# Tokens and weights of both feed-forward layers' first multiplication as pairs of fp16 tiles, with scales found on the chip

## The chip, the cores and the metric

The program runs on one core of a Trainium2 chip. The metric is the device time of the launch in microseconds (us). The core has five engines: TensorE (PE in the profile, its weight loads are PEld), VectorE (DVE), ScalarE (ACT), GpSimd (POOL) and SyncE (SP, which here only issues DMAs). Each works through its own queue in order.

## The reference

Attention with mixing of heads ahead of and behind the softmax, then two feed-forward layers, all in float32. After attention there are 4 x 448 = 1792 tokens of 768 numbers.

```
scores = q @ k^T / 8;  scores = mix_pre(scores);  attn = softmax(scores)
x = mix_post(attn) @ v                       # 1792 x 768
h = x @ w_in;  x = (h * cos(h)) @ w_out      # layer 0: 768 -> 2048 -> 768
g = x @ w_gate;  v = x @ w_val
out = (silu(g) * v) @ w_out2                 # layer 1: 768 -> 1536 -> 768
```

## The kernel before

**Precision.** A float32 product is made from three matmuls of a high and a low part: each operand `a` is split into `hi`, `a` rounded to a type that TensorE takes, and `lo = a - hi`, and `wh*xh + wh*xl + wl*xh` goes into one PSUM tile. In the feed-forward layers both parts are fp32r, a 4-byte type. The softmax and `post` part of attention already uses fp16 parts.

**Attention** runs from 0 to about 515 us as one list of steps for 180 blocks, whose order on every engine is written out by hand (`order`, L360, under `tc.manual_schedule`). In the last chunk of blocks the start of layer 0 is woven in by `early_plan` (L629).

**Feed-forward layers** (`run`, L652). The hidden dimension is cut into groups of 256 columns (8 groups in layer 0, 6 in layer 1), the tokens into 4 tiles `t` of 448. A unit is one group and one token tile: `l1` (L593) makes 2 x 128 hidden columns (`e` = 0, 1), with 18 matmuls of 448 columns each (6 blocks of 128 rows, three products; L567 to L569), in layer 1 twice that, for gate and value (`col`). `hidden` (L571) makes the nonlinearity and splits the result into `gh` and `gl`. `l2` (L600) multiplies it with 2 x 128 rows of the second weight matrix: 6 output tiles `m`, 6 matmuls each (L613 to L615), and each PSUM tile `py` (pool `ps_y`, four buffers) is added into `acc` in SBUF (L619 on VectorE, for the first group a copy on ScalarE, L617). `l2` of a unit stands one unit behind its `l1`. In the last group of layer 0 each finished `acc` tile is split at once into the next layer's tokens (L622, L623).

**Weights** arrive as 64-bit words, the bits of float64 numbers. `w_dma` (L463) loads half a slab, 3 blocks of 128 x 128, into `raw` (three buffers). `w_shift` (L473, ScalarE) scales the upper words, `w_bits` (L482, three VectorE instructions) puts the float32 number together from both words, and `w_split` (L494) makes `hi` (L506, ScalarE) and `lo` (L507, GpSimd). A slab of the first multiplication has key `(layer, "i", col, fi)`, one of the second `(layer, "o", fi)`. The half-built number `f` has two buffers. `load_in` (L514) is written ahead of the unit or units that need it: in layer 0 in the first unit of a group, for the next group; in layer 1 behind the `l2` that follows the last `l1` of a group, right ahead of the next group's first `l1`.

**Order.** Outside the block written by hand, the framework orders each engine's queue while the kernel is built. The place in the program is the priority; an instruction whose inputs are expected later lets later ones pass. What came of it for this kernel is seen in the trace.

**Scale of v.** `scale_v` (L147) finds a power of two for the values `v`, by a maximum, a matmul with `ones` (tile psp, L76), and arithmetic on exponents. `pv_out` (L290) takes it out again (`und`) when attention's result leaves PSUM.

## Time and profile before

| | |
|---|---|
| median of 3 runs | 1530.59 us (1526.16 to 1532.99) |
| the profiled execution | 1526.95 us, span 1525.2 us |
| mean granted clock of TensorE | 0.994 of full speed |
| busy | PE 1452.0, PEld 1199.3, DVE 971.4, ACT 652.4, POOL 632.0 us |
| stages | attention to about 515 us, layer 0 to about 975, layer 1 to the end |

The span goes from the first to the last instruction of the program; the profiled execution took 1.75 us more than that. Times in the rows are counted from the start of the span. The end of a matmul is modelled and neighbours overlap, so the distance from one start to the next, not the duration, says how fast TensorE goes. Releasers, what ended an engine's idle time, are inferred from semaphores.

### The profile page before, as it was taken

To read this page: it belongs to the slowest core of one execution; us is meant where nothing else is said; L and a number is where in the kernel's file an instruction comes from. 1 tells how busy PE (TensorE), PEld (TensorE's weight loads), DVE (VectorE), ACT (ScalarE), POOL (GpSimd) and SP (SyncE) were. 2 spreads that over 40 slices of the span, in tenths; PEclk is the share of its full clock that TensorE was granted. 3 is DMA by queue.
4 is the path that set the end of the run, shared out by engine and by line. 5 is a ranking of instruction groups with operands and counts; after the bars stand their busy time and mean duration, and the time that the engine had idled before them with its cause. 6 is when DMAs were issued, how large, how long until landed. Compare 5 with 4: busy or idle time off the path is not lost.

```text
span 1525.2 us, 26832 instructions
## 1 busy us (share of the span) xinstructions
PE 1452.0 (95%) x10306; PEld 1199.3 (79%) x10306; DVE 971.4 (64%) x1982; ACT 652.4 (43%) x1398; POOL 632.0 (41%) x531
## 2 busy tenths in 40 slices
PE   4799899999998799999999999999999999999999
PEld 2465566565566699999999998998998989899898
DVE  3888788889889684866766767834236263543613
ACT  3677777777776562322322323534313131221310
POOL 1777677777768542432322422313223131321310
PEclk9999999999999999999999999999999999999999
DMA  5445445455445530211202211202102030120202
GB/s 169 132 135 161 141 138 164 142 150 156 137 120 148 149 118 21 84 42 42 83 21 63 65 39 42 82 23 67 58 20 85 21 104 22 55 70 0 73 37 109
DMA packets 93567, 133.04 MB, mean 87 GB/s; under 512 B 18848, under 2 KB 80768, under 8 KB 93440
## 3 DMA queue, kind: packets, MB, share of 16 engines
q1 hardware_dynamic: 93440, 131.34, 29.0%
q8 instruction: 81, 1.33, 0.4%
q14 instruction: 46, 0.38, 0.1%
HBM read 81.59 MB, written 11.01 MB: 61 GB/s over the span
## 4 chain that ended last, share of the span: by engine, by line
PE 57%; DVE 4%; POOL 2%; ACT 1%; issue 1%; ACTq 0%; POOLq 0%
PE ph L568 11%; PE ph L567 11%; PE ph L569 11%; PE py L613 8%; PE py L614 8%; PE py L615 8%; POOL l_i L507 1%; DVE f_i L490 1%; DVE f_i L487 1%; DVE f_i L486 1%; ACT f_i L479 1%; ACT h_i L506 0%; POOL l_o L507 0%; DVE f_o L486 0%; DVE r L589 0%
## 5 line engine op out<-in xcount | busy, mean ns | idle before, releaser
L567 PE MATMUL ph<-x,h_i 128*128 128x448 f32 x960 | 352.5, 367 | 0.0
L569 PE MATMUL ph<-x,l_i 128*128 128x448 f32 x960 | 350.7, 365 | 0.9 <-POOL l_i L507 0.9
L568 PE MATMUL ph<-x,h_i 128*128 128x448 f32 x960 | 350.6, 365 | 0.7 <-POOL x L547 0.7
L591 POOL TENSOR_TENSOR gl<-r,gh 128x448 fp32r<-128x448 f32 x112 | 134.0, 1196 | 498.1 <-ACT gh L590 468.0
L231 POOL TENSOR_SCALAR eh<-e,sm 120x448 f16<-120x448 f32 x180 | 246.7, 1371 | 129.3 <-DVE sm L226 91.0
L613 PE MATMUL py<-gh,h_o 128*128 128x448 f32 x672 | 249.9, 372 | 13.0 <-DVE acc L619 7.9
L615 PE MATMUL py<-gh,l_o 128*128 128x448 f32 x672 | 247.8, 369 | 3.0 <-POOL l_o L507 3.0
L614 PE MATMUL py<-gl,h_o 128*128 128x448 f32 x672 | 247.5, 368 | 0.0
L619 DVE TENSOR_TENSOR acc<-py,acc 128x448 f32<-128x448 f32 x288 | 175.8, 619 | 88.2 <-PE py L615 87.9
L202 PE MATMUL psm<-x,wpre_sb 120*120 120x448 f32 x360 | 179.5, 581 | 15.1 <-ACT e L215 14.9
L568 PEld LDWEIGHTS ph<-x,h_i 128*128 128x128 f32 x960 | 180.3, 188 | 16.2 <-POOL x L547 1.1
L569 PEld LDWEIGHTS ph<-x,l_i 128*128 128x128 f32 x960 | 180.2, 188 | 16.2 <-POOL l_i L507 1.6
L567 PEld LDWEIGHTS ph<-x,h_i 128*128 128x128 f32 x960 | 180.3, 188 | 15.6 <-issue 0.6
L589 DVE TENSOR_TENSOR r<-ph,r 128x448 f32<-128x448 f32 x48 | 29.9, 623 | 198.9 <-PE ph L569 198.7
L613 PEld LDWEIGHTS py<-gh,h_o 128*128 128x128 f32 x672 | 126.5, 188 | 32.0 <-DVE acc L619 13.1
L507 POOL TENSOR_TENSOR l_i<-f_i,h_i 128x384 fp32r<-128x384 f32 x80 | 86.8, 1092 | 139.0 <-ACT h_i L506 139.0
L251 PE MATMUL psa<-wpost,eh 120*112 120x120 f16 x720 | 131.6, 226 | 13.0 <-DVE at L272 10.3
L615 PEld LDWEIGHTS py<-gh,l_o 128*128 128x128 f32 x672 | 126.6, 188 | 15.9 <-POOL l_o L507 4.1
L590 ACT CAST gh<-r 128x448 fp32r<-128x448 f32 x112 | 63.4, 566 | 173.2 <-DVE r L589 135.0
L215 ACT ACTIVATE e<-psm,sm 120x448 f32<-120x448 f32 x180 | 115.2, 640 | 50.5 <-DVE sm L226 48.9
L614 PEld LDWEIGHTS py<-gl,h_o 128*128 128x128 f32 x672 | 126.6, 188 | 11.4
L238 DVE SCALAR_TENSOR_TENSOR el<-e,sm,eh 120x448 f16<-120x448 f32 x180 | 133.4, 741 | 1.4 <-POOL eh L231 1.4
(83 smaller groups left out, 2320.5 us busy)
## 6 DMA issues: line engine op xcount, KB each, us to landing
r_o<-in_w_out SPq DMA_DIRECT2D x56, 384.0 KB
x<-s SPq DMA_DIRECT2D x96, 210.0 KB
r_i<-in_w_in SPq DMA_DIRECT2D x32, 384.0 KB
x<-s SPq DMA_DIRECT2D x48, 192.5 KB
r_i<-in_w_gate SPq DMA_DIRECT2D x24, 384.0 KB
r_i<-in_w_val SPq DMA_DIRECT2D x24, 384.0 KB
x<-s SPq DMA_DIRECT2D x48, 175.0 KB
qr<-in_qT SPq DMA_DIRECT2D x15, 360.0 KB
```

What stands on the lines that cost most here:

```text
L202: nc.tensor.matmul(ps[:120, :S], wpre_sb, X[b, c][:120, k], start=True, stop=True)
L231: nc.gpsimd.tensor_scalar(eh, E[b, c, k], sm[:, 3:4], 1.0, op0=ALU.mult, op1=ALU.mult)
L238: nc.vector.scalar_tensor_tensor(el, E.pop((b, c, k)), sm[:, 3:4], eh, op0=ALU.mult, op1=ALU.subtract)
L251: nc.tensor.matmul(o, eh[:, j], wpost_sb[0], start=True, stop=False)
L567: nc.tensor.matmul(ps, wh, xh, start=(kk == 0), stop=False)
L568: nc.tensor.matmul(ps, wh, xl, start=False, stop=False)
L569: nc.tensor.matmul(ps, wl, xh, start=False, stop=(kk == 5))
L591: nc.gpsimd.tensor_tensor(gl, r, f(gh), op=ALU.subtract)
L613: nc.tensor.matmul(ps, wh, gh[:, e], start=(e == 0), stop=False)
L614: nc.tensor.matmul(ps, wh, gl[:, e], start=False, stop=False)
L615: nc.tensor.matmul(ps, wl, gh[:, e], start=False, stop=(e == 1))
L619: nc.vector.tensor_tensor(acc[:, m], ps, acc[:, m], op=ALU.add)
```

## The change

The tokens X of both layers and the weight slabs of the first multiplication (`"i"`) are now pairs of fp16 tiles. So that the parts keep enough bits, each weight slab and each token tile is brought to a suitable size by a power of two, found on the chip:

- `w_max` takes the largest magnitude of each partition from the upper words of a raw half slab (VectorE). `w_sum` reduces the two halves' maxima to a power of two on each partition and adds these up over the partitions with a matmul of `ones` by one column; `w_unit` cuts the sum to a power of two and makes its inverse, which `w_shift` then uses as scale. So nothing of a slab is built before both its halves have landed and the matmul is through.
- For the tokens of layer 0 the scale is that of v, which `pv_out` now leaves in. For layer 1, `l2` of the last group takes the maximum of each `acc` tile, and `next_x` makes the scale in the same way, behind all six tiles, and then splits them.
- `hidden` takes the scales out again, by a scalar for each partition (`w_by`), in instructions that were there, of which one changes its form.
- One of the four `py` buffers in PSUM becomes the place of the sums (`ps_u`). `raw` (and the other default tiles of its pool) gets five buffers instead of three.
- In `early_plan` the loads and steps of the first two slabs move.

```diff
+    ff.ones = ones
+    ff.ps_sum = lambda name: ps_v.tile([128, 512], F32, tag="pv", name=name)
...
             p = pow2_c(scales[b], 112, f"v{b}")
-            und = const.tile([128, 1], F32, tag="und", bufs=2, name=f"und_{b}")
-            nc.vector.tensor_scalar(und, p[:, 0:1], pw[:, 0:1], 2.0 ** -14, op0=ALU.mult, op1=ALU.mult)
-            vscale[b] = p, und
+            nc.vector.tensor_scalar(
+                ff.unit[0][:, b:b + 1], p[:, 0:1], pw[:, 0:1], 2.0 ** -9, op0=ALU.mult, op1=ALU.mult
+            )
+            vscale[b] = p
...
-        nc.scalar.activation(x, PV.pop((b, c, g3))[:, :3, :n], AF.Copy, scale=vscale[b][1])
+        nc.scalar.activation(x, PV.pop((b, c, g3))[:, :3, :n], AF.Copy, scale=2.0 ** -5)
...
-        self.p_wr = self.pool("m_wr", 3, side="right")
+        self.p_wr = self.pool("m_wr", 5, side="right")
...
-        self.ps_y = self.pool("ps_y", 4, PSUM)
+        self.ps_y = self.pool("ps_y", 3, PSUM)
+        ps_u = self.pool("ps_u", 1, PSUM)
+        self.ps_sum = lambda name: ps_u.tile([128, 512], F32, tag="u", name=name)
...
+    def w_max(self, key, z):
+        if z == 0:
+            self.scale[key] = self.p_unit.tile([128, 6], F32, tag="u", name="u_" + self.nm(key, z))
+        top = self.raw[key, z].bitcast(F32).rearrange("p m (n w) -> p (m n) w", w=2)[:, :, 1]
+        self.tc.nc.vector.tensor_reduce(
+            out=self.scale[key][:, z:z + 1], in_=top, axis=AX.X, op=ALU.max, apply_absolute_value=True
+        )
+    def w_sum(self, key):
+        nc = self.tc.nc
+        u = self.scale[key]
+        m = u[:, 2:3]
+        nc.vector.tensor_scalar(m, u[:, 0:1], u[:, 1:2], 2.0 ** -112, op0=ALU.max, op1=ALU.mult)
+        nc.vector.tensor_scalar(
+            m.bitcast(I32), m.bitcast(I32), 3, 0x7C000000, op0=ALU.logical_shift_left, op1=ALU.bitwise_and
+        )
+        ps = self.ps_sum("su_" + self.nm(key, 0))
+        nc.tensor.matmul(ps[:, 0:1], self.ones, m, start=True, stop=True)
+        self.part["sum", key] = ps
+    def w_unit(self, key):
+        nc = self.tc.nc
+        u = self.scale[key].bitcast(I32)
+        ps = self.part.pop(("sum", key))[:, 0:1].bitcast(I32)
+        nc.vector.tensor_scalar(u[:, 3:4], ps, 0x7C000000, None, op0=ALU.bitwise_and)
+        nc.vector.tensor_scalar(
+            u[:, 4:5], u[:, 3:4], 3, 31 << 23, op0=ALU.logical_shift_right, op1=ALU.bitwise_xor
+        )
...
         t = self.p_wr.tile([128, 3, 128], F32, tag="f", bufs=2, name="f_" + self.nm(key, z))
-        nc.scalar.activation(t, top, AF.Copy, scale=2.0 ** -112)
+        by = self.scale[key][:, 4:5] if key[1] == "i" else 2.0 ** -112
+        nc.scalar.activation(t, top, AF.Copy, scale=by)
         self.part[key, z] = t
...
+            kind = F16 if key[1] == "i" else F32R
             self.W[key] = tuple(
-                pool.tile([128, 6, 128], F32R, tag=tag + p, name=p + "_" + self.nm(key, z)) for p in "hl"
+                pool.tile([128, 6, 128], kind, tag=tag + p, name=p + "_" + self.nm(key, z)) for p in "hl"
             )
+            if key[1] == "i" and (key[0] == 0 or key[3] > 1):
+                self.w_by(key)
         hi, lo = (w[:, 3 * z:3 * z + 3] for w in self.W[key])
         t = self.part.pop((key, z))
         nc.scalar.copy(hi, t)
-        nc.gpsimd.tensor_tensor(lo, t, f(hi), op=ALU.subtract)
+        nc.gpsimd.tensor_tensor(lo, t, hi if key[1] == "i" else f(hi), op=ALU.subtract)
+    def w_by(self, key, t=None):
+        nc = self.tc.nc
+        layer = key[0]
+        if t in (None, 0):
+            self.by[key] = self.p_unit.tile([128, 2, 4], F32, tag="by", bufs=6, name="by_" + self.nm(key, 0))
+        ts = slice(0, 4) if t is None else slice(t, t + 1)
+        for i, c in enumerate((0.5, 0.5 * INV2PI) if layer == 0 else (0.5,)):
+            nc.vector.tensor_scalar(
+                self.by[key][:, i, ts], self.unit[layer][:, ts], self.scale[key][:, 3:4], c,
+                op0=ALU.mult, op1=ALU.mult,
+            )
...
     def load_w(self, key):
+        if key[1] == "i":
+            for step in (self.w_dma, self.w_max):
+                for z in range(2):
+                    step(key, z)
+            self.w_sum(key)
+            self.w_unit(key)
         for z in range(2):
-            for step in (self.w_dma, self.w_shift, self.w_bits, self.w_split):
+            if key[1] == "o":
+                self.w_dma(key, z)
+            for step in (self.w_shift, self.w_bits, self.w_split):
                 step(key, z)
...
-            x = self.p_x.tile([128, 12, S], F32R, tag="x", name=f"x{layer}_{t}")
+            x = self.p_x.tile([128, 12, S], F16, tag="x", name=f"x{layer}_{t}", padded_shape=[128, 24, S])
...
-            self.p_hl[t].tile([128, 6, S], F32R, tag=f"hl{z}", name=f"x{layer}{z}_{t}") for z in range(2)
...
-        eng.tensor_tensor(lo, self.raw.pop(("x", t, m)), f(hi), op=ALU.subtract)
...
+            by, turn = (self.by[0, "i", 0, 2 * g + e][:, i, t:t + 1] for i in range(2))
...
-            nc.vector.tensor_scalar(k, ps, INV2PI, 0.25, op0=ALU.mult, op1=ALU.add)
-            nc.vector.scalar_tensor_tensor(r, ps, INV2PI, k, op0=ALU.mult, op1=ALU.subtract)
+            nc.vector.tensor_scalar(k, ps, turn, 0.25, op0=ALU.mult, op1=ALU.add)
+            nc.vector.scalar_tensor_tensor(r, ps, turn, k, op0=ALU.mult, op1=ALU.subtract)
...
-            nc.vector.tensor_tensor(r, ps, r, op=ALU.mult)
+            nc.vector.scalar_tensor_tensor(r, ps, by, r, op0=ALU.mult, op1=ALU.mult)
         else:
-            nc.scalar.activation(r, self.PH[e, 0], AF.Silu)
-            nc.vector.tensor_tensor(r, self.PH[e, 1], r, op=ALU.mult)
+            if g == 0:
+                for col in range(2):
+                    self.w_by((1, "i", col, e), t)
+            by = [self.by[1, "i", col, 2 * g + e][:, 0, t:t + 1] for col in range(2)]
+            nc.scalar.activation(r, self.PH[e, 0], AF.Silu, scale=by[0])
+            nc.vector.scalar_tensor_tensor(r, self.PH[e, 1], by[1], r, op0=ALU.mult, op1=ALU.mult)
...
-            self.x_new(1, t)
+            mx = self.p_unit.tile([128, 8], F32, tag="mx", bufs=2, name=f"mx_{t}")
...
             if last and layer == 0:
-                hi, lo = (x[:, m] for x in self.X[1, t])
-                nc.scalar.copy(hi, acc[:, m])
-                nc.vector.tensor_tensor(lo, acc[:, m], f(hi), op=ALU.subtract)
+                nc.vector.tensor_reduce(
+                    out=mx[:, m:m + 1], in_=acc[:, m], axis=AX.X, op=ALU.max, apply_absolute_value=True
+                )
             elif last:
...
+        if last and layer == 0:
+            self.next_x(t, acc, mx)
+    def next_x(self, t, acc, mx):
+        nc = self.tc.nc
+        self.x_new(1, t)
+        u, by = mx[:, 6:7], mx[:, 7:8]
+        nc.vector.tensor_reduce(out=u, in_=mx[:, :6], axis=AX.X, op=ALU.max)
+        ps = self.ps_sum(f"sx_{t}")
+        nc.tensor.matmul(ps[:, 0:1], self.ones, u, start=True, stop=True)
+        nc.vector.tensor_scalar(u, ps[:, 0:1], 2.0 ** -100, 2.0 ** 100, op0=ALU.max, op1=ALU.min)
+        nc.vector.tensor_scalar(u.bitcast(I32), u.bitcast(I32), 0x7F800000, None, op0=ALU.bitwise_and)
+        nc.vector.tensor_scalar(self.unit[1][:, t:t + 1], u, 2.0 ** -14, None, op0=ALU.mult)
+        nc.vector.reciprocal(by, self.unit[1][:, t:t + 1])
+        for m in range(6):
+            hi, lo = (x[:, m] for x in self.X[1, t])
+            nc.scalar.activation(hi, acc[:, m], AF.Copy, scale=by)
+            nc.vector.scalar_tensor_tensor(lo, acc[:, m], by, hi, op0=ALU.mult, op1=ALU.subtract)
...
-        wi = (0, 0, 0, 0), (1, 3, 6, 8)
+        wi = (0, 0, 1, 2), (3, 4, 6, 8)
...
             plan.append((s + wi[0][k], self.w_dma, key, z))
+            plan.append((s + wi[0][k] + 1, self.w_max, key, z))
+            if z:
+                plan.append((s + wi[0][k] + 2, self.w_sum, key))
+                plan.append((s + wi[0][k] + 3, self.w_unit, key))
```

## Rows read from the trace of the kernel before

**Rows 1.** The page, busy time and share of each engine.

```profile
PE 1452.0 (95%) x10306; PEld 1199.3 (79%) x10306; DVE 971.4 (64%) x1982; ACT 652.4 (43%) x1398; POOL 632.0 (41%) x531
```

**Rows 2.** Windows: stretch, its length; busy us (instructions) per engine, clock, DMA share, GB/s.

```profile
455.00:505.00 50.00, 43.56 (x549) 32.14 (x548) 46.06 (x101) 32.93 (x75) 38.30 (x29) 0.97 0.50 149
555.00:870.00 315.00, 315.00 (x1536) 286.96 (x1534) 213.19 (x379) 100.77 (x186) 99.72 (x87) 1.00 0.19 58
945.00:1005.00 60.00, 60.00 (x295) 54.95 (x294) 49.43 (x90) 29.55 (x55) 17.46 (x15) 1.00 0.20 61
1005.00:1045.00 40.00, 40.00 (x198) 36.84 (x197) 2.50 (x4) 10.19 (x19) 4.63 (x4) 1.00 0.03 10
```

**Rows 3.** Waits of PE over the run: us in total, times, longest.

```profile
PE py L613 <- DVE acc L619: 7.9, 10, 1.0
```

**Rows 4.** The page, groups: count | busy us, mean ns | idle before, releaser.

```profile
L567 PE MATMUL ph<-x,h_i 128*128 128x448 f32 x960 | 352.5, 367 | 0.0
```

**Rows 5.** Timeline of PE in layer 1, then layer 0: start us, us.

```profile
1089.81 0.36 PE L568 MATMUL ph<-x,h_i 128*128 128x448 f32 x1
...
1090.21 0.36 PE L567 MATMUL ph<-x,h_i 128*128 128x448 f32 x1
...
623.68 0.37 PE L569 MATMUL ph<-x,l_i 128*128 128x448 f32 x1
...
624.72 0.37 PE L568 MATMUL ph<-x,h_i 128*128 128x448 f32 x1
```

**Rows 6.** Timeline of PE, `post` of one block: first and last of twelve.

```profile
41.46 0.22 PE L251 MATMUL psa<-wpost,eh 120*112 120x120 f16 x1
...
42.04 0.22 PE L253 MATMUL psa<-wpost,el 120*112 120x120 f16 x1
```

**Rows 7.** Timeline of PE around the sum for v's scale.

```profile
43.95 0.37 PE L76 MATMUL psp_v<-diag_v,ones 112*128 112x112 f32 x2
44.25 0.68 PE L186 MATMUL pss<-k,q 64*120 64x448 f32 x4
```

**Rows 8.** Groups of DVE instructions by form.

```profile
L140 DVE TENSOR_REDUCE vmx<-vm 112x1 f32<-112x768 f32 x16 | 15.1, 943 | 0.5 <-DMA vm<-in_vN 0.5
...
L584 DVE SCALAR_TENSOR_TENSOR r<-ph,k 128x448 f32<-128x448 f32 x64 | 39.7, 620 | 1.5
...
L222 DVE TENSOR_SCALAR sm<-sm 120x1 f32<-120x1 f32 x180 | 26.4, 147 | 56.9 <-ACT e L215 56.7
```

**Rows 9.** Timeline of DVE and PE in two bursts of layer 0.

```profile
616.34 1.14 DVE L619 TENSOR_TENSOR acc<-py,acc 128x448 f32<-128x448 f32 x2
...
616.49 0.37 PE L613 MATMUL py<-gh,h_o 128*128 128x448 f32 x1
...
631.78 0.61 DVE L619 TENSOR_TENSOR acc<-py,acc 128x448 f32<-128x448 f32 x1
...
631.30 0.37 PE L613 MATMUL py<-gh,h_o 128*128 128x448 f32 x1
```

**Rows 10.** Timeline at a change of group in layer 1, and DVE later.

```profile
1046.28 1.99 POOL L507 TENSOR_TENSOR l_i<-f_i,h_i 128x384 fp32r<-128x384 f32 x2 [8.85 <-ACT h_i L506]
...
1047.33 0.55 ACT L479 ACTIVATE f_i<-r_i 128x384 f32<-128x384 f32 x1 [0.28 <-POOL l_i L507]
...
1050.49 1.02 POOL L507 TENSOR_TENSOR l_i<-f_i,h_i 128x384 fp32r<-128x384 f32 x1 [2.23 <-ACT h_i L506]
...
1063.88 1.33 POOL L507 TENSOR_TENSOR l_i<-f_i,h_i 128x384 fp32r<-128x384 f32 x1
...
1065.53 0.36 PE L615 MATMUL py<-gh,l_o 128*128 128x448 f32 x1
1065.73 0.36 PE L567 MATMUL ph<-x,h_i 128*128 128x448 f32 x1
...
1089.43 0.58 DVE L486 TENSOR_SCALAR f_i<-f_i 128x384 int32<-128x384 int32 x1 [8.12 <-ACT f_i L479]
```

**Rows 11.** The chain that ended last: start us, us, what.

```profile
1135.78 1.02 POOL l_i L507
```

More of the change, by code (lines that the diff above doesn't have):

```diff
@@ L61, in attention @@
     ps_m = pool("ps_m", 2, PSUM, mixed)
-    ones = const.tile([128, 128], F32, name="ones")
+    ones = ff.p_const.tile([128, 128], F32, name="ones")
     nc.vector.memset(ones, 1.0)
@@ L164, in split_v @@
         rv = r.rearrange("p (m e d) -> p m e d", e=2, d=D)
-        by = vscale[b][0][:112, 1:2]
+        by = vscale[b][:112, 1:2]
         if part == 0:
@@ L358, in attention @@
         at(i, fn, *a)
-    order = ("at_hi","l1_part","post","spread","dma_v","w_bits","hidden","den","rowmax","rec","norm_hi","dma_k","x_dma","w_dma","pv_out","at_lo","norm_lo","lo_k","dma_q","max_v","w_shift","lo_q","split_v","x_lo","premix","scale_v","w_split","expo","x_hi","qk","hi_k","hi_q","pv")
+    order = ("at_hi","l1_part","post","spread","dma_v","w_sum","w_unit","w_bits","hidden","den","rowmax","rec","norm_hi","dma_k","x_dma","w_dma","pv_out","at_lo","norm_lo","lo_k","dma_q","max_v","w_max","w_shift","lo_q","split_v","x_lo","premix","scale_v","w_split","expo","x_hi","qk","hi_k","hi_q","pv")
     with tc.manual_schedule():
@@ L422, in __init__ @@
         self.p_x = self.pool("m_x", 2)
+        self.p_const = self.pool("m_const", 1)
+        self.p_unit = self.pool("m_unit", 4)
+        self.unit = [self.p_const.tile([128, 4], F32, name=f"unit{layer}") for layer in range(2)]
+        self.scale, self.by = {}, {}
         cols = [w.rearrange("(k p) n -> p k n", p=128) for w in (w_in, w_gate, w_val)]
@@ L530, in x_new @@
         self.X[layer, t] = tuple(
-            self.p_hl[t].tile([128, 6, S], F32R, tag=f"hl{z}", name=f"x{layer}{z}_{t}") for z in range(2)
+            self.p_hl[t].tile([128, 6, S], F16, tag=f"hl{z}", name=f"x{layer}{z}_{t}") for z in range(2)
         )
@@ L546, in x_lo @@
         eng = self.tc.nc.vector if t and m % 2 else self.tc.nc.gpsimd
-        eng.tensor_tensor(lo, self.raw.pop(("x", t, m)), f(hi), op=ALU.subtract)
+        eng.tensor_tensor(lo, self.raw.pop(("x", t, m)), hi, op=ALU.subtract)
     def load_x(self, t):
```

## Prediction, made before the changed kernel was run

> **What bounds the kernel now.** I read the page first: its busy line and its clock line say whether one engine fills the span. TensorE (PE) is busy for 1452.0 of 1525.2 us, nobody else for more than two thirds [rows 1]. Busy time flatters PE, because the records of pipelined matmuls overlap, so next I read busy time by stretch [rows 2]. From 555 to 870 us PE has no gap at all, at the full granted clock, and runs 1536 matmuls in 315 us, 205 ns each. The attention tail (455 to 505) is another stage: there PE has gaps and VectorE (DVE) is busy for 46.06 of 50 us. Third, the waits of PE: over the whole run the largest total in the feed-forward layers is 7.9 us, behind the additions into `acc` [rows 3]. So in the feed-forward layers, about two thirds of the run, the spacing of the matmuls sets the time. What matters is the step from one start to the next, not the recorded duration (367 ns).
>
> **The matmuls that change.** The first multiplication has 3 x 960 = 2880 matmuls of 448 columns (three lines, L567 to L569, of which one row is shown) [rows 4]. Their starts lie 200 ns apart in a quiet stretch of layer 1 (two steps from 1089.81 to 1090.21) and 208 ns apart in a busy one of layer 0 (623.68 to 624.72: five steps in 1.04 us) [rows 5]. I take 203.5, near the middle. The trace has no fp16 matmul of this width, but `post` has fp16 ones of 120 columns, each with a weight load of its own: 11 steps in 0.58 us (41.46 to 42.04), 52.7 ns each [rows 6]. 120 columns at the granted 2.4 GHz are 50 ns, so an fp16 matmul with its load costs 2.7 ns beside its columns, where a 4-byte one costs 13 to 21 ns beside 186.7. An fp16 matmul of 448 columns should come to 52.7 + 328 / 2.4 = 189.4 ns. Bounds: 186.7 (columns alone), and 200 to 208 (no change). Gain: 2880 x (203.5 - 189.4) = 40.6 us; from 0 to 49.
>
> One rule speaks against that. The `post` rows show 52.7 ns with a new weight tile each time. The Trainium skill ("TensorE: Matmul & The Clock Gate", section "Weight-path perf modes — Fast Weight Load (FWL) and DoubleRow") says that the array takes one element per cell and cycle whatever its width, and that the weight load goes by columns and not bytes; the same section says that a faster weight load is on for 128 weights of a type that isn't FP32. By the first sentence alone nothing is gained; by the second the load shrinks. The measured 4-byte step of 200 to 208 is longer than its columns, and the `post` step isn't, so the trace sides with the second.
>
> **What PE gets in addition.** One sum over partitions for each of 40 weight slabs (16 in layer 0, 24 in layer 1) and for each of 4 token tiles: `ones` (128x128, f32) against one column. The nearest rows are the two psp records: the first starts at 43.95, the next other matmul at 44.25, 0.30 us [rows 7]. They move 112 columns twice (2 x 47 ns); without these some 0.2 us stay. 44 x 0.2 = 8.8 us; bounds 2 x 53 ns (two smallest steps with a load each, 4.7 us in all) and 0.30 us (13.2).
>
> **What DVE gets.** Each half slab a maximum over 384 elements. A reduction of 768 takes 943 ns and an instruction on one element 147 [rows 8]; that is 1.04 ns an element, so 147 + 384 x 1.04 = 0.55 us, x 80 = 44 us. The token maxima (448) are 24 x 0.61 = 15 us. Small instructions: 4 for each slab (160), 68 for `w_by`, 20 in `next_x`, at 0.15 us [rows 8], 38 us. Together 97 us on 971 [rows 1]. The operations of `hidden` and `next_x` that change form keep their price: with one operand from PSUM, the fused form (L584) takes 620 ns and the plain addition (L619) 0.61 us [rows 8, 9]. ScalarE and GpSimd get the same counts with 2-byte outputs: nothing, and ScalarE's idle time would cover some. Where is DVE's cover? From 555 to 870 it is idle for 102 of 315 us [rows 2], and the new work there (some 4 us for each of 5 to 6 pairs of slabs) fits. Two places lack cover:
> - Attention tail: 4 halves and 2 slabs fall in it, 2.2 + 12 x 0.15 = 4 us, against 3.9 us of idle DVE [rows 2]. I take 3 us (0 to 4); the new maxima also wait for DMAs that only ScalarE waited for, with rowmax behind them on DVE.
> - Between the layers: `next_x` and the token maxima bring 15 + 3 us, while DVE is idle for 10.6 of 60 us from 945 to 1005, and for 37.5 of 40 behind that [rows 2]. 7 us have no cover at once, the rest can slide. I take 5 us (0 to 8).
>
> **Three PSUM buffers for py instead of four.** With three, the fourth tile of `l2` waits for the first tile's addition. In two bursts of one group I can read that off: the fourth tile's first matmul starts at 616.49, the first tile's addition at 616.34 (two end at 617.48, so the first near 616.9), 0.4 us late; in the second burst they are at 631.30 and 631.78 (to 632.39), 1.1 us late [rows 9]. For 7 groups of layer 0 that is 7 x 1.5 = 10.5 us, 12 with some room. I take 6: a PE that has waited once lets DVE catch up, and five raw buffers instead of three let the work on the slabs spread. In layer 1 the present waits behind `acc` grow by at most one tile (1.23 us) at each of 5 changes of group; I take 4 us (0 to 6).
>
> **The longer chain to a weight slab.** Maximum, sum, unit, then as before. In layer 1 a slab set's splitting begins at 1046.28 (GpSimd's first l_i) and ends with the one at 1063.88 (1.33 long); the matmuls that use it begin at 1065.73 [rows 10]. The last slab is needed only after three quarters of 14 us more. The chain grows by about 2 us a slab (two maxima, four small instructions, a turn on PE), 8 us for four, and the slack of over 10 us hides it, if its sums run as early as the trace shows other steps to run: the bit work at 1089.43 belongs to a group whose splitting the chain of waits shows at 1135.78 [rows 10, 11]. I take 2 us (0 to 4). SP's queue has the same DMAs, no more; the maxima now hold up only what comes later on DVE.
>
> **Sum.** -40.6 + 8.8 + 3 + 5 + 6 + 4 + 2 = -11.8 us, on the profiled execution's 1526.95 us (1.75 beside its span): 1515.2. The three timed runs have a median of 1530.59, 3.6 above it, and that difference is no property of the change; I give 1517, in between and nearer to the sum.
>
> **Rivals.**
> - *The sum waits for its place on PE (slower).* Everywhere in layer 1, PE goes in program order: the second multiplication ends with its matmul at 1065.53, the next unit's first starts at 1065.73 [rows 10]. `load_in` for the next group of layer 1 stands right ahead of the unit that needs it. If PE never runs dry earlier, the sums run only there, and splitting starts there and not 18 us earlier. From then: 0.7 us (sum, unit) + 4.1 (ScalarE shift, three DVE steps, cast, GpSimd: 1047.33 to 1051.51) + 17.9 (1047.33 to 1065.21, six halves more [rows 10]) = 22.7 us to the last half. PE has 7.4 us of `l2` and about 12 us of `l1` ahead of that, so it waits 3 us, and the three further sums wait for DVE in its busiest stretch, another 2. Six changes of group: 30 us, less the 2 above: 1545. It decides from a start later than 19 us ahead of the last need. For it: PE's gapless order. Against: DVE's and ScalarE's queues do run ahead.
> - *DVE gives everything back (no change).* The buffer and boundary terms at their upper bounds (12 + 6 + 8 + 4) and the sums at 13.2: -40.6 + 13.2 + 30 + 2 = +4.6, 1532. For it: DVE's back-to-back rows in bursts [rows 9].
> - *Half the gain.* The 4-byte step of a quiet stretch is 200, and what disturbs the busy one stays: 2880 x 10.6 = 30.5 us instead of 40.6: 1527.
> - *The type doesn't matter.* The change then doesn't bring what it could: 1517 + 40 = 1557. Against it: the `post` step [rows 6]. The skill's sentence on element width is this rival.
> - *All covers hold*: -40.6 + 4.7 + 3 = -33, 1494 to 1498.
>
> **From these to the numbers.** Chances: forecast 0.40, sum at its place 0.24, DVE gives all back 0.13, half the gain 0.12, type 0.05, covers 0.06. The forecast itself spans 1508 to 1526; the range, with the first rival inside and the last two mostly outside, is 1499 to 1548. A measurement tells about 0.5% (7.6 us) from no change. Faster: 0.35 of the forecast, 0.06, 0.04 of the half gain, 0.02: 0.47. Slower: 0.21 of the first rival, 0.05 of the type, 0.06 of DVE: 0.32. Same: 0.21.
>
> **What would show it.** In the profile after, starts of the first multiplication's matmuls about 189 ns apart (over 198: the type rival). Two sum records and about 0.2 us beside the stream. Waits of PE on `acc` of 15 to 20 us in all (more: DVE). Waits of the sum matmul or of ph on l_i: a few us; at about 5 us each at 1/6 of layer 1, the first rival. DVE near 1070 us busy. The prediction is wrong if PE's waits in layer 1 exceed 15 us, or if the step isn't below 195 ns.

## The result: slower, 1.0132 times the time before, and the profile after

The changed kernel takes 1549.01 us (median of 4, 1547.83 to 1551.89) against 1528.8 us of the kernel before, run beside it: ratio 1.0132, 95% interval 1.0103 to 1.0162. The forecast was 1517 with a range up to 1548. Its profiled execution took 1547.83 us, with a span of 1545.7.

I read the views in the order of the prediction. The busy line of the page, answering to [rows 1]:

```profile
PE 1436.3 (93%) x10394; PEld 943.8 (61%) x10394; DVE 1048.3 (68%) x2334; ACT 663.8 (43%) x1398; POOL 622.0 (40%) x531
```

PE is less busy than before in a longer span, weight loads have shrunk by 255 us, and DVE has 77 us more, where the prediction said 97. Busy time by stretch, the same stretches and columns as [rows 2], changed kernel:

```profile
555.00:870.00 315.00, 297.02 (x1482) 207.32 (x1480) 223.90 (x433) 98.01 (x174) 87.33 (x81) 0.98 0.17 51
945.00:1005.00 60.00, 58.30 (x295) 43.68 (x294) 50.69 (x106) 19.80 (x35) 11.11 (x10) 1.00 0.00 1
1005.00:1045.00 40.00, 34.41 (x165) 17.66 (x166) 36.81 (x92) 21.01 (x38) 16.52 (x15) 0.91 0.41 118
```

In the stretch of layer 0 where PE had no gap, it now has 18 us of them and starts 54 matmuls fewer. The clock has a part in the fewer starts: behind 520 us the trace has TensorE at 1.2 GHz for 20.5 us, before for 3.4. The longest such stretch, 10.2 us from 590 us on, lies behind waits for an out slab. Two windows of it (columns as above; 0.50 of the clock is 1.2 GHz):

```profile
585.00:590.00 5.00, 2.85 (x14) 1.59 (x13) 4.52 (x8) 2.08 (x5) 2.28 (x2) 1.00 0.52 158
595.00:600.00 5.00, 3.98 (x11) 2.63 (x11) 3.89 (x7) 1.74 (x3) 3.24 (x3) 0.50 0.41 122
```

So look at what PE waits for. Waits of PE in the changed kernel from 520 us on (total us, times, longest):

```profile
PE ph L638 <- POOL l_i L555: 13.8, 32, 0.8
PE py L687 <- ACT h_o L554: 11.2, 13, 2.5
PE py L689 <- POOL l_o L555: 7.4, 13, 1.9
PE py L687 <- DVE acc L693: 6.9, 8, 1.3
PE ph L636 <- ACT h_i L554: 4.3, 2, 4.1
```

Before, the largest was `acc` with 7.9 [rows 3], and these two, 6.7 us in all, were the waits on weight slabs:

```profile
PE py L613 <- ACT h_o L506: 3.7, 1, 3.7
PE py L615 <- POOL l_o L507: 3.0, 3, 2.1
```

`acc` hasn't grown. The waits on weight slabs have, to 36.7 us. Those in layer 0 (18.6 us) are all on out slabs (`h_o`, `l_o`), those in layer 1 (18.1) all on in slabs (`h_i`, `l_i`), the ones that now need a sum. The matmuls themselves do what was forecast. PE's timeline in layer 0, changed kernel, first and last of fourteen:

```profile
757.72 0.35 PE L637 MATMUL ph<-x,h_i 128*128 128x448 f16 x1
...
760.18 0.35 PE L638 MATMUL ph<-x,l_i 128*128 128x448 f16 x1
```

13 steps in 2.46 us are 189.2 ns each; before it was 200 to 208 [rows 5]. Over the run, the mean step between starts (disturbed ones of 215 ns and more left out) is 189.7 ns in layer 0 and 189.5 in layer 1, against 203.2 and 202.6.

Why the slabs are late is seen where the sums lie. Timeline of the changed kernel in layer 0, DVE, PE and ACT, for the two in slabs of one group:

```profile
716.10 0.54 DVE L488 TENSOR_REDUCE u_i<-r_i 128x1 f32<-128x384 f32 x1
...
728.57 0.54 DVE L488 TENSOR_REDUCE u_i<-r_i 128x1 f32<-128x384 f32 x1
...
760.37 0.28 PE L503 MATMUL su_i<-u_i,ones 128*128 128x1 f32 x2
...
761.24 0.15 DVE L512 TENSOR_SCALAR u_i<-su_i 128x1 int32<-128x1 int32 x1
...
761.61 0.28 PE L503 MATMUL su_i<-u_i,ones 128*128 128x1 f32 x2
...
762.72 0.63 ACT L524 ACTIVATE f_i<-r_i,u_i 128x384 f32<-128x384 f32 x1
```

All maxima are there at 729, and the small steps behind them at 731. The sums run at 760.37 and 761.61, behind the first `l1` of the group, which is the place of `load_in` in the program. For over 30 us nothing of the slabs can be built; then eight halves, the out slabs' among them, go through ACT, DVE and POOL at once, and PE waits for the out slabs, which it needs first. In layer 1 the sums lie behind an `l2` (1180.87 and 1182.11, then 1191.99 and 1195.81), and the `l1` that uses the slabs runs beside their building. PE's and POOL's timeline there:

```profile
1180.87 0.28 PE L503 MATMUL su_i<-u_i,ones 128*128 128x1 f32 x2
...
1190.93 0.36 PE L638 MATMUL ph<-x,l_i 128*128 128x448 f16 x1 [0.39 <-POOL l_i L555]
...
1202.93 0.36 PE L638 MATMUL ph<-x,l_i 128*128 128x448 f16 x1 [0.61 <-POOL l_i L555]
...
1203.94 1.28 POOL L555 TENSOR_TENSOR l_i<-f_i,h_i 128x384 f16<-128x384 f32 x1 [1.06 <-ACT h_i L554]
1205.27 0.36 PE L638 MATMUL ph<-x,l_i 128*128 128x448 f16 x1 [0.47 <-POOL l_i L555]
```

The splitting of the set ends at 1205, 24 us behind the first sum. Before, it began 19 us ahead of the first use [rows 10]. This is what the first rival described for layer 1. Its 1545 comes nearest of all, but by luck, as the account of the steps below shows; and the late sum isn't the whole cause, as the experiments show.

### The profile page after: what moved, and what is told of

The parts are those of the page before. It is cut to its first block, busy times and chain, and to the rows that moved or that the text cites. A ratio compares the mean times of both kernels' runs of the same rounds, so it can differ in the third digit from the quotient of the medians.

```text
span 1545.7 us, 27273 instructions
## 1 busy us (share of the span) xinstructions
PE 1436.3 (93%) x10394; PEld 943.8 (61%) x10394; DVE 1048.3 (68%) x2334; ACT 663.8 (43%) x1398; POOL 622.0 (40%) x531
## 4 chain that ended last, share of the span: by engine, by line
PE 44%; DVE 7%; POOL 5%; ACT 3%; issue 2%; DMA 0%; POOLq 0%; DVEq 0%; ACTq 0%; SPq 0%
PE ph L638 9%; PE ph L636 8%; PE ph L637 8%; PE py L689 6%; PE py L687 6%; PE py L688 6%; POOL l_i L555 3%; DVE f_i L532 2%; ACT f_i L524 1%; ACT h_i L554 1%; DVE f_i L531 1%; DVE f_i L535 1%; POOL l_o L555 1%; DVE f_o L532 1%; POOL gl L665 1%
## 5 line engine op out<-in xcount | busy, mean ns | idle before, releaser
L638 PE MATMUL ph<-x,l_i 128*128 128x448 f16 x960 | 340.4, 355 | 18.3 <-POOL l_i L555 18.2
L636 PE MATMUL ph<-x,h_i 128*128 128x448 f16 x960 | 341.9, 356 | 7.2 <-ACT h_i L554 4.3
L665 POOL TENSOR_TENSOR gl<-r,gh 128x448 fp32r<-128x448 f32 x112 | 134.2, 1198 | 526.0 <-ACT gh L664 522.9
L637 PE MATMUL ph<-x,h_i 128*128 128x448 f16 x960 | 340.5, 355 | 0.7 <-DVE x L616 0.7
L687 PE MATMUL py<-gh,h_o 128*128 128x448 f32 x672 | 256.6, 382 | 20.2 <-ACT h_o L554 11.2
L638 PEld LDWEIGHTS <-l_i 128*128 128x128 f16 x960 | 94.4, 98 | 120.7 <-POOL l_i L555 34.7
L636 PEld LDWEIGHTS <-h_i 128*128 128x128 f16 x960 | 95.1, 99 | 98.1 <-issue 14.2
L663 DVE SCALAR_TENSOR_TENSOR r<-ph,by_i,r 128x448 f32<-128x448 f32 x48 | 32.7, 680 | 177.5 <-PE ph L638 177.5
L637 PEld LDWEIGHTS <-h_i 128*128 128x128 f16 x960 | 94.4, 98 | 84.2 <-issue 6.2
L555 POOL TENSOR_TENSOR l_i<-f_i,h_i 128x384 f16<-128x384 f32 x80 | 77.5, 977 | 149.9 <-ACT h_i L554 145.8
L200 ACT COPY s<-pss 120x448 f32<-120x448 f32 (+2 forms) x192 | 96.8, 536 | 83.2 <-DMA x<-s 34.0
```

The source lines that it names most:

```text
L555: nc.gpsimd.tensor_tensor(lo, t, hi if key[1] == "i" else f(hi), op=ALU.subtract)
L636: nc.tensor.matmul(ps, wh, xh, start=(kk == 0), stop=False)
L637: nc.tensor.matmul(ps, wh, xl, start=False, stop=False)
L638: nc.tensor.matmul(ps, wl, xh, start=False, stop=(kk == 5))
L665: nc.gpsimd.tensor_tensor(gl, r, f(gh), op=ALU.subtract)
L687: nc.tensor.matmul(ps, wh, gh[:, e], start=(e == 0), stop=False)
```

## The experiments

Several runs change one thing and see the loss move elsewhere, so the explanations came one behind another. The expectations name them by letters. A: the sums' place alone. B: VectorE's added work itself. C: three `py` buffers. D: a burst of slab work is paid once, in slabs when they are late or in `acc` when they are early. E and H: in that burst the two `f` buffers chain the engines. F: the loss sits in PE's own pace. The others are explained where they stand. "Before" in each comparison was run beside the experiment. The framework orders all queues anew for each kernel, so a small edit also moves other instructions, and a difference of a few us between two kernels has that in it. Of the code only the lines that matter are shown; `...` stands for others.

**e1, no sums for the slabs.** The changed kernel with the fixed scale of the kernel before for slabs; their maxima, sums and scales are left out. The tokens' stay.

```diff
-        by = self.scale[key][:, 4:5] if key[1] == "i" else 2.0 ** -112
+        by = 2.0 ** -112
...
```

> The changed kernel with a fixed scale for the weight slabs (2^-112, as the second multiplication has it) in place of the one found on the chip: maxima, sums and units of the 40 slabs are left out, the tokens' scales stay. Theory A (the sums sit at their place in the program on PE, the weight slabs start late, PE waits for them): the waits on l_i, h_o, l_o and h_i (18.2 + 11.2 + 7.4 + 4.3 = 41 us) fall to about 8 as before, the 40 sums go too (6 us): 1549 - 33 - 6 = about 1510. Rival B (VectorE's added work holds up everything): most of the 97 us of VectorE work goes, so about 1510 as well; e2_unused tells A and B apart. Rival C (three py buffers): they stay, so not under 1535.

Measured: 1544.0 us, 1.0101 [1.006, 1.0141]. Only 5 us came back. PE's waits in e1, from 520 us on:

```profile
PE py L683 <- DVE acc L689: 37.7, 20, 4.9
PE py L683 <- ACT acc L687: 7.0, 4, 4.7
```

The slabs are in time, and now PE waits as long for the additions, for a free `py` buffer. Theory A alone has fallen, and with it B's 1510; C's bound, not under 1535, holds.

**e2, sums made but not used.** Slabs built with the fixed scale as in e1; maxima, sums and scales still computed.

> The changed kernel in which maxima, sums and units of the weight slabs are all computed as before, but the slabs are built with the fixed scale: the work stays, nothing of a slab waits for it. Theory A: near e1_fixed, 1510 to 1520, the waits on weight slabs at some 8 us. Rival B (the work itself): near the changed kernel, 1540 to 1550. Rival C (three py buffers): 1540 to 1550, waits of PE on acc unchanged.

Measured: 1577.27 us, 1.0308 [1.0269, 1.0348]: slower than with their use, and above what any of the three theories gave. PE waits 27.5 us for `acc` and 21.5 us at the sums, in 8 places, for DVE to read the sum before (`su` has one place in PSUM). A sum ties DVE and PE to each other in both directions.

**e4, four py buffers**, the sums taking one of these in turn.

```diff
-        self.ps_y = self.pool("ps_y", 3, PSUM)
-        ps_u = self.pool("ps_u", 1, PSUM)
-        self.ps_sum = lambda name: ps_u.tile([128, 512], F32, tag="u", name=name)
+        self.ps_y = self.pool("ps_y", 4, PSUM)
+        self.ps_sum = lambda name: self.ps_y.tile([128, 512], F32, tag="y", name=name)
```

> The changed kernel with four py buffers again: the sums take one of these in turn instead of a bank of their own. Theory A: 1543 to 1549, as PE waits only 6.9 us on acc. Rival C (three buffers are the loss): 1525 to 1535. Rival B: 1545 to 1549.

Measured: 1596.53 us, 1.044 [1.0403, 1.0478]. PE waits 39.8 us for `h_i` and `l_i`, 23.8 for out slabs, 7.4 at the sums. None of the theories had this. TensorE is at 1.2 GHz for 69.8 us, in the changed kernel for 50.0; that is worth 10 us at most. Why it is so much worse than the changed kernel I didn't settle.

**e5, sums early.** Loads, maxima, sums and scales written one unit (layer 0) or two (layer 1) ahead; six raw buffers, three instead of five for the raw token chunks; three py.

```diff
...
+            if L == 0 and t == 3 and g + 2 < FF1 // 256:
+                self.scale_in(0, g + 2)
+            if t == 2 and i + 2 < len(seq) and seq[i + 2][0] == 1:
+                self.scale_in(1, seq[i + 2][1])
...
```

> The changed kernel with loads, maxima, sums and units of a group's slabs written one unit earlier in layer 0 (ahead of the last unit of the group before the previous place) and two units earlier in layer 1, with six raw buffers; nothing else moves, all work stays. Theory A: the slabs are built as early as in the kernel before; waits on l_i, h_o, l_o, h_i fall from 41 to 10 to 15 us: 1515 to 1522. Rivals B and C: the work and the buffers stay, 1543 to 1552.

Measured: 1557.66 us, 1.0178 [1.0147, 1.0209]. PE waits 30.0 us for `acc`, 7.2 at the sums, 2.2 for in slabs. As in e1: early slabs, and the time goes to `acc`. A's 1515 to 1522 has fallen once more.

**e3, the kernel before with three py buffers**, nothing else.

```diff
-        self.ps_y = self.pool("ps_y", 4, PSUM)
+        self.ps_y = self.pool("ps_y", 3, PSUM)
```

> The kernel before with three py buffers instead of four, nothing else. Theory D (a burst of slab building has to be paid once: PE waits for slabs where these start late, as in the changed kernel, or for the additions behind them where they start early and py has three buffers, as in e1_fixed; only early slabs and four buffers together avoid both): slabs are early here, so waits on acc rise from 9 to 30 to 40 us: 1552 to 1562. Theory A alone (late slabs): at most 1538.

Measured: 1553.28 us beside 1529.74, 1.0156 [1.0132, 1.018]. The buffer given to the sums costs 23.5 us by itself, within D's range; the prediction had 10. PE's waits in e3:

```profile
PE py L613 <- DVE acc L619: 18.9, 22, 2.2
PE py L613 <- ACT acc L617: 5.9, 5, 2.7
```

**e8, no slab sums and four py buffers**: e1, with the tokens' sums in a `ph` buffer (`self.ps_h[0].tile(..., tag="h")`).

> The changed kernel with the fixed scale for weight slabs (as e1_fixed) and with four py buffers; the four sums for the tokens go into a buffer of the ph tiles. Theory D: early slabs and four buffers, both waits small, and the step of 187 ns in the first multiplication shows: 1544 less most of 45 us, 1500 to 1508. Rival B (the loss is what scales and tokens add on VectorE, whatever the buffers): 1530 or more.

Measured: 1530.85 us, 1.0004 [0.9983, 1.0024]. Both suspects are gone and still the 38 us of the type are eaten; D has fallen in its size, and B's forecast, 1530 or more, is met. PE's waits on `acc` from 530 us on:

```profile
PE py L682 <- DVE acc L688: 24.8, 13, 3.7
```

One of these, at a change of group in layer 1, timeline of e8 (PE, DVE, ACT):

```profile
1145.48 0.55 ACT L523 ACTIVATE f_i<-r_i 128x384 f32<-128x384 f32 x1 [2.33 <-POOL l_i L554]
...
1147.83 0.56 ACT L523 ACTIVATE f_i<-r_i 128x384 f32<-128x384 f32 x1 [0.86 <-POOL l_i L554]
...
1150.19 0.55 ACT L523 ACTIVATE f_i<-r_i 128x384 f32<-128x384 f32 x1 [1.40 <-POOL l_i L554]
...
1151.77 1.15 DVE L534 SCALAR_TENSOR_TENSOR f_i<-r_i,f_i 128x384 int32<-128x384 int32 x1
...
1154.39 0.61 DVE L688 TENSOR_TENSOR acc<-py,acc 128x448 f32<-128x448 f32 x1
...
1155.05 0.47 PE L682 MATMUL py<-gh,h_o 128*128 128x448 f32 x1 [3.67 <-DVE acc L688]
```

The reader is to see a ring. `f` has two buffers, so ACT's scaling of a half waits for POOL's subtraction of the half two before it, and the halves follow at 2.36 us. DVE's instructions for a half lie in between, and in DVE's queue the additions into `acc` stand behind the last half. The first addition comes at 1154.39; PE has filled four buffers and stands for 3.67 us.

**e9, four py, all sums in ph buffers, late as in the change.**

> The changed kernel with four py buffers; all sums go into a buffer of the ph tiles, so that no bank is lost and none of the py buffers is taken in turn. Theory D: slabs still late, so the waits on l_i, h_o, l_o, h_i (41 us) stay, the 9 on acc go: 1538 to 1546. Rival C (the buffers alone): 1510 to 1520.

Measured: 1581.2 us, 1.0338 [1.0304, 1.0371], far above what D and C gave. TensorE is at 1.2 GHz for 105.4 us, 55 more than in the changed kernel, worth 28 us at most. PE waits 35.6 us at the sums for DVE's `u_i`, one time 11.85 us: the sum stands ahead of ready work in PE's queue and its maxima stand in DVE's.

**e11, all the change's work, early as e5, four py, one sum for two slabs in a ph buffer.**

> The changed kernel with all its work, four py buffers (sums in a buffer of the ph tiles), loads and sums of a group's slabs written earlier as in e5_early, and one sum for two slabs (20 sums instead of 38 behind attention, and half the small VectorE instructions). Theory D: 1504 to 1515, under both kernels. Rival B (VectorE's work): 1530 or more. Theory A without the buffers: about 1520.

Measured: 1534.64 us, 1.0029 [1.0001, 1.0057]. 14.4 us better than the change, but no gain over before. D's 1504 to 1515 is missed, B's 1530 or more met again. PE waits 20.7 us on `acc`, 11.6 at the sums.

**e12, e8 with four f buffers.**

```diff
-        t = self.p_wr.tile([128, 3, 128], F32, tag="f", bufs=2, name="f_" + self.nm(key, z))
+        t = self.p_wr.tile([128, 3, 128], F32, tag="f", bufs=4, name="f_" + self.nm(key, z))
```

> The kernel of e8 (fixed scale for the weight slabs, four py buffers, sums of the tokens in a ph buffer) with four f buffers instead of two. In e8 one half of a slab follows the other at 2.36 us in layer 1, because ACT's scaling of a half waits for POOL's subtraction of the half two before it; DVE's own work in that is 2.08 us. Theory E (the burst in which a group's slabs are built holds up the additions behind it): with four f the halves follow at 2.1 us, a burst of 8 is 2 us shorter, PE's waits on the additions fall from 28 to 15-22 us: 1520-1528 us. Rival F (the loss sits in PE's own pace after the change of type, not in the queues): no change, 1529-1533.

Measured: 1492.51 us, 0.9745 [0.9717, 0.9772]: 38 us less than e8, several times what E had said, so its direction held and its size didn't. F has fallen, and B for e8, since VectorE has the same work in both (2094 instructions). PE's waits from 530 us on in e12:

```profile
PE py L682 <- DVE acc L688: 7.3, 12, 1.2
PE sx L708 <- DVE mx L706: 2.1, 2, 1.4
```

17.5 of the 38 us are waits on `acc`, 3.6 the one on ACT's `acc`, 1.8 `sx`: 23 in all. The long waits also leave PE at its lower clock behind them. Granted clock in e8 ahead of the wait shown above and 2 us behind it (the number after the busy times):

```profile
1149.00:1153.00 4.00, 2.38 (x12) 1.85 (x10) 3.69 (x6) 1.04 (x3) 2.40 (x2) 1.00 0.70 182
1157.00:1158.00 1.00, 1.00 (x4) 0.91 (x4) 1.00 (x3) 0.51 (x1) 0.00 (x0) 0.50 0.00 0
```

0.50 is 1.2 GHz. Over the run the trace has 51.0 us at this level in e8, 31 of them in seven stretches between 540 us and the end; e12 has 21.0 us, and none there. 30 us less at half the pace are worth 15 at most, which is about what was missing. The changed kernel has 50.0, before 19.4.

**e13, spread.** All the change's work. fp16 slabs are half as large, so four pools of two hold the in slabs of two layer-1 groups. Slabs are built a pair at a time through the units, sums stand behind the `l1` one unit after their maxima, token sums of layer 1 a unit later. Two f, six raw, four py. The core, against e11's order:

```diff
...
+            if pairs and t in (1, 2) and pairs[t - 1]:
+                self.pair_sum(pairs[t - 1])
             if i:
                 self.l2(*seq[i - 1])
             if t == 0 and i:
-                self.load_out(L, g)
+                self.load_out(L, g, (1,))
...
+            if pairs and t in (1, 2) and pairs[t - 1]:
+                self.pair_load(pairs[t - 1])
+            if pairs and t < 2 and pairs[t]:
+                self.pair_top(pairs[t])
+            if t == 3 and new:
+                self.load_out(new[0], new[1], (0,))
```

> All work of the change (maxima, sums, scales), four py buffers, sums in ph buffers, two slabs to a sum. The fp16 slabs are half as large, so that four pools of two hold the in slabs of two whole layer-1 groups instead of one, and the building is spread: pair of slabs number 1 of the next group while units 1 runs, pair 2 in unit 2, one out slab in unit 3, the other in unit 0; maxima a unit before, the sum behind the l1 of the unit in between; the token sums of layer 1 a unit later. Theory E: no burst is left over 4 halves (9.5 us of a unit of 21), so waits of PE on acc and on slabs fall to some 15-25 us in all: first multiplication 532 + second 405 to 413 + sums 6 + waits 20 = 965 to 975, behind an attention of 526 or less: 1497-1510 us. Rival F (PE's own pace): 1525-1535 as e11.

Measured: 1508.07 us, 0.9842 [0.9816, 0.9868], as E said. Waits on `acc` 13.6 us, on slabs 3.3.

**e14, e13 with three f buffers.**

> e13 with three f buffers instead of two. Theory E: 0 to 5 us less than e13, since no burst is longer than its unit: 1495-1508 us. Rival F: as e11, 1525-1535.

Measured: 1496.69 us, 0.9765 [0.974, 0.979]; 11 us less than e13, more than E's 0 to 5. `acc` 6.2 us.

**e16, the kernel before with the order of e13 as far as it has room.**

> The kernel before (4-byte slabs, no sums, four py) with its slabs built in the order of e13 as far as its buffers allow: layer 0 in slabs in unit 2 instead of unit 0, one out slab in unit 3 and one in unit 0; in layer 1 the in slabs stay where they are, since a second set of 4-byte slabs (24 kB a partition) has no room. Theory E: only 17.6 us of waits to win, of which layer 0 has the smaller part: 1518-1530 us. Rival G (the order is worth as much without the change): 1505-1515 us.

Measured: 1535.45 us, 1.0028 [1.001, 1.0046]. As much of the order as has room gains nothing without the change: rival G has fallen for that part, and E's 1518 to 1530 is missed too. What the spread of layer 1's in slabs would bring without the change, no run shows.

**e17, the kernel before with four f buffers; e18, the changed kernel with four f buffers; e19, e9 with four; e21, e11 with four.** Each is the one line of e12. Theories I to K stand in the texts.

> The kernel before with four f buffers instead of two, nothing else. Theory H (two f buffers tie ACT's scaling of a slab half to POOL's subtraction of the half two before it; the chain costs time only where PE comes to the slabs and additions as early as the fp16 multiplication lets it): before has 17.6 us of stalls in its feed-forward layers, of which the chain has a part: 1520-1530 us. Rival I (the two f buffers cost the kernel before as much as e8, some 38 us): 1490-1500.

> The changed kernel with four f buffers instead of two, nothing else: three py buffers and the sums at their late places remain. Theory H: the late sums still hold the slabs back, but behind a sum the halves follow at DVE's pace: 15 to 30 us of the 41 us of waits on slabs go: 1520-1535 us. Rival J (place of the sums alone decides, e4 and e9 had shown that it weighs): 1542-1550.

> e9 (four py buffers, sums in ph buffers at their late places) with four f buffers. Theory H: 1510-1535, far below e9's 1581; rival J (place of the sums): 1565-1581.

> e11 (all work, loads, maxima and sums a unit or two early, four py buffers, two slabs to a sum) with four f buffers. Theory H: as e12 against e8, 25 to 38 us less than e11, and a few us more than e12 for the sums and the end of the attention: 1496-1510 us. Rival K (e12 gained because nothing but slabs was in the queues; the maxima and scales of this kernel take it back): 1520-1535.

Measured: e17 1529.43, 0.9992 [0.9977, 1.0008]: no change, so I has fallen. In its profiled execution the stretch from the 73rd matmul of the feed-forward layers to the last is 4.7 us shorter (1001.9 instead of 1006.6 us) and starts 5.5 us later; so the ring costs the kernel before some 5 us at most. e18 1563.56, 1.024 [1.0214, 1.0266]: 15 us *slower* than the changed kernel; neither H nor J had that. Its waits on slabs are 47.1 us instead of 36.7, and TensorE is at 1.2 GHz for 74.8 us instead of 50.0. e19 1565.43, 1.0249 [1.0202, 1.0297]: J. e21 1521.21, 0.9945 [0.9921, 0.9969]: 13 us less than e11; by the total, H's size fails and K has it. But in the two profiled executions the stretch from the 73rd matmul on falls by 26.4 us (1008.0 to 981.6), as H said, and starts 7.3 us later. There the waits on `acc` fall from 20.7 to 7.7 us, and those at the sums stay (11.6 and 11.7). With the sums late, more `f` buffers bring 16 us (e9 to e19) or cost 15 (e18). e18's timeline at a change of group in layer 1 shows how the sum holds DVE, too:

```profile
1188.00 0.14 DVE L499 TENSOR_SCALAR u_i<-u_i 128x1 int32<-128x1 int32 x1
...
1192.42 0.28 PE L503 MATMUL su_i<-u_i,ones 128*128 128x1 f32 x2
1192.73 0.16 DVE L512 TENSOR_SCALAR u_i<-su_i 128x1 int32<-128x1 int32 x1 [4.58 <-PE su_i L503]
...
1199.85 0.36 PE L638 MATMUL ph<-x,l_i 128*128 128x448 f16 x1 [2.55 <-POOL l_i L555]
```

DVE has the maxima at 1188 and stands idle for 4.58 us until PE comes to the sum in its own order, 3.0 us of them at 1.2 GHz; PE then waits 2.55 us for the slab that DVE couldn't build.

**e22, e13 with four f buffers** and five buffers for the raw token chunks (e13 had three); **e23, e22 with three py buffers** and the sums in a place of their own, as the change has it.

> e14 (the changed kernel with all its maxima, sums and scales, its slabs built pair by pair through the units, four py buffers) with four f buffers instead of three, and five xr buffers for the token chunks instead of three. Theory L (three separate covers have to hold at once: sums out of the way, py buffers, f buffers): 1490-1497 us, a few us under e14, from the end of the attention (e14's first l2 at 524.7 us of the span, e12's at 516.8). Rival M (e14 is at the end of what this order gives): 1495-1500.

> e22 with three py buffers and a PSUM place of their own for the sums, as the change has it. Theory L (the covers are separate, and three buffers cost what they cost the kernel before in e3): e22 plus 15 to 25 us: 1508-1520 us. Rival N (three buffers cost time only beside a long burst of slab work, and the spread has none): within 5 us of e22.

Measured: e22 1488.66 us (1487.61 to 1489.37), 0.9727 [0.9708, 0.9745]: 42 us faster than before and 60 faster than the change, with all its maxima, sums and scales; a little below L. So VectorE's added work isn't the loss: DVE is busy for 1045.1 us here and for 1048.3 in the changed kernel. B has fallen. e23 1502.42, 0.9823 [0.98, 0.9845]. Three buffers cost 13.8 us here, just under L's 15 to 25; N has fallen. PE's waits from 525 us on, in e22:

```profile
PE py L714 <- DVE acc L720: 6.1, 7, 2.7
PE py L716 <- POOL l_o L571: 1.7, 2, 1.4
PE sx L744 <- ACT r L689: 1.4, 1, 1.4
```

And in e23:

```profile
PE py L715 <- DVE acc L721: 17.8, 11, 3.0
PE py L715 <- ACT acc L719: 2.8, 3, 2.2
```

PE in most of layer 1 (columns as above), first in the kernel before:

```profile
1070.00:1435.00 365.00, 358.20 (x1752) 328.05 (x1751) 166.46 (x271) 88.21 (x170) 88.87 (x81) 1.00 0.18 52
```

Then in e22, which has no gap and starts 144 matmuls more in the same time:

```profile
1070.00:1435.00 365.00, 365.00 (x1896) 242.19 (x1895) 192.05 (x360) 93.22 (x173) 93.73 (x85) 1.00 0.16 49
```

## Why the prediction was wrong, by its steps

From the starts of PE's matmuls, the time of one group (us; mean of layer 0's groups 2 to 5 and of layer 1's groups 1 to 4), and the time from the 73rd matmul of the feed-forward layers, the first behind the two `l1` that `early_plan` weaves into attention, to the last. A group is counted from there on, as 288 matmuls in layer 0 and 432 in layer 1, the first with number 0. A cover is what hides a piece of work from PE: idle time of an engine, or a free buffer.

| | before | change | e12 | e22 |
|---|---|---|---|---|
| layer 0, one group | 59.1 | 61.2 | 57.7 | 57.3 |
| layer 1, one group | 90.1 | 88.3 | 85.3 | 83.9 |
| 73rd to last | 1006.6 | 1022.8 | 967.8 | 962.1 |

- *Step of the fp16 matmul* (-40.6): right. 189.7 and 189.5 ns against 189.4; 1152 x 13.5 + 1728 x 13.1 = 38.2 us. The 4-byte step outside of quiet stretches is what I had taken. The rival that the type doesn't matter has fallen. The rows of weight loads agree: 98 ns a record for fp16 and 188 for the 4-byte type. Here the measurement sides with the second sentence that the prediction weighed from the Trainium skill ("TensorE: Matmul & The Clock Gate", section "Weight-path perf modes — Fast Weight Load (FWL) and DoubleRow"), the faster weight load for types other than FP32, and against the first, by columns and not bytes.
- *Sums on PE* (+8.8): right as PE's own time. From 1180.66 to 1181.49 three 4-byte steps take 0.83 us with a sum in between and 0.60 without: 0.23 a sum, 10 us for 44. As a point where PE and DVE wait for each other they cost more: 21.5 us in e2, 35.6 in e9.
- *Attention tail* (+3): the 73rd matmul starts 4.3 us later, the first of `l2` 5.9 (526.0 instead of 520.2). *Boundary* (+5): the last group of layer 0 takes 50.1 us instead of 45.3, +4.8, and the first of layer 1 another 3.2 more.
- *Three py buffers* (+10): mis-sized. 23.5 us in e3, 13.8 in e23. I had read the rhythm of two quiet bursts [rows 9] and let the loss end there. In the profile of the change it isn't seen at all: there PE already stands for the slabs, and only in e1, where these are in time, does the wait on `acc` come up.
- *The longer chain to a weight slab* (+2): **this is the step that failed**, at the condition "if its sums run as early as the trace shows other steps to run". DVE's steps do run ahead, and the maxima did (716 to 729). The sum is a matmul on the engine that has no gap, and it ran where the program has it. 36.7 us of waits on slabs came of it, where before there were 6.7. The sign that the prediction set for itself shows it, too: PE's waits in layer 1 are 21.6 us, over its 15. The first rival had this for layer 1 alone, at 30 us; layer 0, where the sums have to wait for their place too, takes 2 us a group more than before instead of 2 less. By that rival's terms (-24.4 for the step, 4.8 for sums, 4 for buffers, 30 for waits) layer 1 should have become 14 us longer, and layer 0 about 1 us shorter. Counted from the 73rd matmul, layer 1 became 4.4 us shorter and layer 0 20.7 longer, 7.6 of these in its group 1, where the clock fell. Two errors of some 20 us cancel: its 1545 is luck.

Two terms the prediction didn't have at all. The matmuls of `l2`, which the change leaves alone, go faster by some 9 us (2016 steps of 200.7 ns instead of 205.3, see the last section). And TensorE is at its lower clock for 17 us more behind 520 us, worth 8.5 us at most. So beside the 20 us by which the kernel is slower, the type's 38 and the 9 of `l2` are eaten as well.

What no part of the prediction had either is that the terms aren't added: no single cure brings the loss back: without sums 5 us (e1), four py buffers -32 or -48 (e9, e4), four f buffers -15 (e18). PE waits for whichever cover ends last, and the next one stands close behind. The covers are three, each shown by a pair of runs in which the others hold: the place of sums and slabs, the f ring (e8 to e12: 38; e13 to e14: 11), and the fourth py buffer (e23 to e22: 13.8). For the place (e19 to e22, both with four py and four f: 77 us) the edit is the largest: 44 us come with the sums early and paired (e21), 33 more with the spread, two more pools for the in slabs and five buffers for raw token chunks (e22), where the waits at slab sums fall from 11.7 to 1.3 us. What each of these parts is worth alone, no run shows. I had said of DVE that its idle time covers the new work; its total was indeed smaller than forecast. The order in its queue was the cost. Before, the same two f buffers cost some 5 us at most (e17), behind the change 38 (e8 to e12). That the faster PE makes the difference, as it comes to the slabs sooner, is argued; the two kernels also differ in raw buffers and in the order of their queues.

The type's 38 us and the 9 of `l2` are 47 together, and e22 is 42 faster than before: its maxima, sums and scales cost some 5 us net. Two things stay open. Why four py buffers make the kernel with late sums worse (e4, e9), beyond the waits and the clock named, and how much of the differences between kernels is the queues' new order rather than the edit.

## What to carry to other kernels

When the engine that sets the pace gets faster, every cover is to be computed anew against the new pace: buffers in the feeding chain that cost little before can cost as much as the change brings. A small operation put on the busiest engine in the middle of a preparation runs at its place in that engine's order, and not when its inputs are there; write it one unit ahead of its users, with the work that needs it spread over the units behind. If a change halves the size of a tile, the room that it frees is the first candidate to pay for that.

## What the runs showed of the hardware that I had not expected

The 4-byte matmuls of `l2`, which nothing changed, run at two paces, by program and not by load. The mean step (below 215 ns) is 200.9 and 200.5 ns (layer 0 and 1) in the changed kernel and 200.4 in e22, and 205.3 in the kernel before, 205.6 and 204.0 in e8. PE's timeline in the changed kernel, first and last of sixteen matmuls (15 steps, 200 ns each):

```profile
1177.66 0.36 PE L689 MATMUL py<-gh,l_o 128*128 128x448 f32 x1
...
1180.66 0.37 PE L689 MATMUL py<-gh,l_o 128*128 128x448 f32 x1
```

And in e8 (15 steps, 205 ns each):

```profile
1146.93 0.36 PE L682 MATMUL py<-gh,h_o 128*128 128x448 f32 x1
...
1150.00 0.36 PE L682 MATMUL py<-gh,h_o 128*128 128x448 f32 x1
```

5 ns on 2016 matmuls are 10 us; the changed kernel and e22 have them beside the gain of the type, e12 hasn't. All kernels without slab sums (before, e1, e3, e8, e12, e16, e17) have the slow pace and all with them the fast one, but for e5 (204.8 and 203.8), so the sums themselves don't decide. I suspect where the tiles lie; no run here tells.

The last bit operation of a half takes 0.55 us on DVE alone and 1.16 beside POOL's subtraction, which then has 1.29 instead of 0.91 (e8: DVE at 1139.55 and 1147.05, POOL at 1140.77 and 1146.51). At 1140.77 POOL came first: it kept its 0.91, and DVE's instruction at 1141.08 took 1.03. The Trainium skill ("SBUF — State Buffer", section "SBUF: two separate sides") has DVE and GpSimd share one pair of ports as an exclusive lock for instructions with two inputs from SBUF; these rows agree. It lengthens just the burst that the additions stand behind.
